# Linear attention and a cosine FFN on one core: keys' maxima subtracted by TensorE in 4 units where it was 7, with a new order table

## The chip, the core and the metric

The kernel runs on one core of a Trainium2 chip. The metric is the device time of one execution in microseconds (us). The kernel before takes 993.45 us, the median of 3 runs (992.97 to 993.52).

## The reference, cut to what matters

```python
def phi(x):                                    # q, k: 8 x 8 x 576 x 64, w_phi: 64 x 128
    proj = einsum('bhsd,df->bhsf', x, w_phi)
    proj = proj - max(abs(proj), axis=-1)      # one maximum for each row of 128 features
    return concatenate([exp(proj), exp(-proj)])
kv  = einsum('bhsf,bhsd->bhfd', phi(k), v);  z = sum(phi(k), axis=2)
out = einsum('bhsf,bhfd->bhsd', phi(q), kv) / (einsum('bhsf,bhf->bhs', phi(q), z) + 1e-6)
x = out, heads side by side                    # 4608 x 512
h = x @ w_in;  g = h * cos(h);  y = g @ w_out  # w_in: 512 x 2048, w_out: 2048 x 512
```

The data are float32. The matmuls of the attention run on float32 as it is (two records of the trace for one matmul); those of the FFN split every operand into a high and a low part and multiply three of the four pairs.

## The kernel before, in words

**Work.** The attention is cut into 32 units (`attention(u)`, L518), each with two heads of one batch. The FFN (`visit`, L795, and `visit_two`, L962) takes 512 rows of x at a time, which four units have to deliver. So nothing of the FFN can start until the first four units are stored and the first weights are converted to their two parts.

**One unit** is a set of steps on the engines:

- PE (TensorE): `q_mm` (L548, two matmuls) and `q_end` (L551) project the queries; `k_mm` (L594, eight matmuls into two banks) and its tail (L619) project the keys; `kv_mm` (L698 and L704) makes kv; two `x_mm` (L733, the second with L739) multiply it by the queries.
- ACT (ScalarE): `q_copy` (L559 twice, L561) empties the query banks; `exp_k` (L649 or L652) and `exp_q` (L658, four instructions) are the exponentials; `kv_out` (L710) copies kv.
- DVE (VectorE): the maxima of the queries (L565 to L574, L583), those of the keys (`k_max`, L632), `k_neg` (L635), and the division and transposition of the result (L745 to L761).
- POOL (GpSimd): the subtraction of the queries' maxima (L579, L587).

**The keys' maxima.** A unit's keys stand in two full banks of 128x512 and a small tail. In a unit of `K_SUMS` (L307) the maximum of the two full banks is subtracted on PE by one more matmul into the bank (`k_sub`, L640, its own shape in the list of shapes), after which one ACT instruction (L649) takes exp of the whole bank, once for +x and once for -x. In all other units there is no `k_sub`: DVE makes the negated maximum (`k_neg`, L635), and ACT subtracts it as a bias. A bias holds for 128 columns alone, so a bank then takes 8 instructions of 128x128 (L652) and not 2 of 128x512. The tail goes by bias in every unit.

```python
597        eqs, eqb = [], []
598        on_pe = (0, 1) if u in K_SUMS else ()
...
640            PE.matmul(out=pv, lhsT=minus, rhs=d["mk", i].unsqueeze(2).broadcast_to([P, n, P]), start=False, stop=True,
641                      skip_group_check=True)
...
647            for s in range(2):
648                if i in on_pe:
649                    ACT.activation(out=e[:, :, s * P:(s + 1) * P], in_=pk, func=AF.Exp, scale=1.0 - 2.0 * s)
650                    continue
651                for g in range(n):
652                    ACT.activation(out=e[:, g, s * P:(s + 1) * P], in_=pk[:, g, :], func=AF.Exp, scale=1.0 - 2.0 * s,
653                                   bias=d["lk" if s == 0 else "mk", i][:, g:g + 1])
...
671            if i in on_pe:
672                kms[i] = Step("PE", 0.86, lambda i=i: k_sub(i), [kms[i]], use=[kb[i], pks[i]], kind="a.k_sub")
673            else:
674                kms[i] = Step("DVE", 0.1, lambda i=i: k_neg(i), [kms[i]], use=[pks[i]], port=True, kind=phase + "k_neg")
```

**Order.** Every piece of work is a `Step`; there are 3839. The table `ORDER` (L89 to L235) lists them by number, and `plan()` (L238) issues them in that order: it alone decides how the steps stand in each engine's queue, and it gives out the eight PSUM banks in turn. Each engine works through its queue in order and waits at an instruction whose inputs or buffers are not free. The costs in the `Step`s do nothing at run time. ACT loads a table whenever it goes from exp to sin or back (ACT_TABLE_LOAD). PE's order mixes four shapes of matmul.

Of the kernel before, what the change touches and what calls it, by code (L numbers as in the profile page):

```python
# [26 lines left out]
def phi_attention_then_cos_ffn(ctx: ExitStack, tc: tile.TileContext, qkT, vS, w_phi, w_in, w_out, out, outT):  # L27
# [42 lines left out]
    class Step:  # L70
        def __init__(self, eng, cost, fn, deps=(), take=(), use=(), lat=None, table=None, port=False, kind="", pipe=0.0):
# [10 lines left out]
            for b in self.take + self.use:  # L82
# [6 lines left out]
    ORDER = [0, 3, 5, 4, 7, 8, 6, 9, 42, 58, 10, 11, 1, 44, 59, 46, 18, 60, 1265, 45, 64, 23, 61, 65, 66, 12, 48, 62, 17, 63, 19, 21, 13, 1266, 47, 24, 20, 68, 22,  # L89
# [148 lines left out]
    def plan():  # L238
# [6 lines left out]

        for x in (steps[i] for i in ORDER):
            for b in x.take:
# [56 lines left out]

    GROUP = 3
    Q_DVE = range(0)
    K_SUMS = range(7)  # L307
    WARM = 7
    WHOLE = 8
    W_POOL = ()  # L310
# [1187 lines left out]
```

## Time and profile before

| | |
|---|---|
| median of 3 runs | 993.45 us (992.97 to 993.52) |
| the profiled execution | 991.67 us, of which the span of its instructions is 989.9 us |
| granted TensorE clock | 1.000 over the span |
| PE busy | 982.2 us, 99% |
| PE weight loads | 796.5 us, 80% |
| DVE busy | 854.8 us, 86% |
| ACT busy | 788.3 us, 80% |
| POOL busy | 203.8 us, 21% |
| DMA | 211.67 MB, 214 GB/s on average |

Read it from the busy shares to the stages: an average of 80% for ACT covers stretches in which it is hardly ever idle and others in which a third of its time is free. The tables by stretch in the section on rows show which. [...]

### The profile page before, as it was taken

The page shows a single profiled execution, that of the slowest core. Times are in us where ns is not written, and L with a number is a line of the kernel's source. Part 1 is how long each engine was busy: PE and PEld are TensorE (multiplying, and loading weights), DVE is VectorE, ACT ScalarE, POOL GpSimd, SP SyncE. Part 2 cuts the span into 40 slices and gives each one's busy share as a digit, 9 for nine tenths or more (in the row PEclk, how much of TensorE's full clock was granted, in tenths as well). Part 3 has the DMA queues.
Part 4 walks back from the last instruction along what each step waited for, and adds up shares of the span by engine and source line. Part 5 has one row for each costly group of instructions (what it writes and reads, how often), then busy time and mean ns, then how long its engine had stood idle before and what let it go on. Part 6 is the DMA issues. An engine that isn't in the chain of part 4 may idle for free.

```text
span 989.9 us, 22350 instructions
## 1 busy us (share of the span) xinstructions
PE 982.2 (99%) x8586; PEld 796.5 (80%) x8586; DVE 854.8 (86%) x1494; ACT 788.3 (80%) x1559; POOL 203.8 (21%) x295
## 2 busy tenths in 40 slices
PE   9999999999999999999999999999999999999998
PEld 6778888888888888887778877788888888888886
DVE  7999999998899987877988679999886899776977
ACT  6899999878678868979998879788867776766663
POOL 4664442323232122201123210222000100000000
PEclk9999999999999999999999999999999999999999
DMA  7766865947587583777665746776566486664665
GB/s 259 211 211 194 264 208 177 339 136 234 191 280 247 181 285 126 237 248 275 214 195 174 227 148 203 231 256 212 179 204 214 151 262 189 242 226 160 181 191 191
DMA packets 118746, 211.67 MB, mean 214 GB/s; under 512 B 18672, under 2 KB 61808, under 8 KB 118640
## 3 DMA queue, kind: packets, MB, share of 16 engines
q1 hardware_dynamic: 118496, 210.18, 65.1%
q8 instruction: 67, 1.10, 0.4%
q14 instruction: 39, 0.32, 0.1%
q10 hardware_dynamic: 144, 0.07, 0.0%
HBM read 149.39 MB, written 60.82 MB: 212 GB/s over the span
## 4 chain that ended last, share of the span: by engine, by line
PE 88%; DVE 6%; ACT 2%; DMA 1%; issue 1%; POOL 1%; SPq 1%; DVEq 0%; ACTq 0%; POOLq 0%
PE bank L1293 22%; PE bank L1090 22%; PE bank L860 12%; PE bank L698 5%; PE bank L733 5%; PE bank L907 4%; PE bank L909 4%; PE bank L908 4%; PE bank L594 3%; PE bank L548 2%; PE bank L704 1%; ACT ek L652 1%; DMA qk<-qkT 1%; PE bank L640 1%; DVE m L565 1%
## 5 line engine op out<-in xcount | busy, mean ns | idle before, releaser
L587 POOL TENSOR_TENSOR pq<-pq,bq 128x288 f32<-128x288 f32 x128 | 122.1, 983 | 111.8 <-DVE bq L583 100.9
L652 ACT ACTIVATE ek<-bank,mk 128x128 f32<-128x128 f32 x464 | 128.1, 406 | 6.7 <-DVE mk L635 5.8
L1293 PE MATMUL bank<-gh,wo_l 128*128 128x512 f32 x336 | 104.8, 393 | 0.2
L1293 PE MATMUL bank<-gh,wo_h 128*128 128x512 f32 x336 | 104.9, 393 | 0.0
L579 POOL COPY m<-m 32x36 f32<-32x36 f32 x96 | 30.1, 314 | 331.7 <-DVE m L574 307.4
L658 ACT ACTIVATE eq<-pq 128x576 f32<-128x576 f32 x128 | 81.1, 711 | 4.4 <-POOL pq L587 3.4
L1202 ACT ACTIVATE g<-g,halfpi 128x512 f32<-128x512 f32 x96 | 67.5, 718 | 18.9 <-DVE g L1199 18.5
L1090 PE MATMUL bank<-xh_t,wi 128*128 128x512 f32 x192 | 75.8, 395 | 0.7 <-ACT bank L1108 0.7
L733 PEld LDWEIGHTS bank<-kv,eq 128*64 128x64 f32 x2048 | 63.8, 138 | 13.1 <-issue 3.9
L1293 PEld LDWEIGHTS bank<-gh,wo_l 128*128 128x128 f32 x336 | 62.3, 188 | 14.5 <-ACT gh L50 1.1
L1293 PEld LDWEIGHTS bank<-gh,wo_h 128*128 128x128 f32 x336 | 62.2, 188 | 13.5 <-issue 0.5
L733 PE MATMUL bank<-kv,eq 128*64 128x65 f32 x2048 | 69.7, 223 | 0.0
L698 PEld LDWEIGHTS bank<-vs,ek 128*64 128x64 f32 x2048 | 62.5, 138 | 8.7 <-issue 2.6
L1199 DVE SCALAR_TENSOR_TENSOR g<-g,hs 128x512 f32<-128x512 int32 x72 | 51.5, 723 | 17.8 <-ACT g L1196 17.3
L1293 PE MATMUL bank<-gl,wo_l 128*128 128x512 f32 x168 | 66.1, 394 | 0.6 <-DVE gl L55 0.6
L698 PE MATMUL bank<-vs,ek 128*64 128x65 f32 x2048 | 66.4, 223 | 0.2 <-DVE g_qk L1209 0.2
L1293 PE MATMUL bank<-gl,wo_h 128*128 128x512 f32 x168 | 65.6, 390 | 0.0
L632 DVE TENSOR_REDUCE mk<-bank 128x4 f32<-128x512 f32 (+1 forms) x96 | 50.6, 542 | 8.3 <-PE bank L594 8.3
L907 PE MATMUL bank<-wo_h,gh 128*128 128x512 f32 x144 | 57.7, 401 | 0.0
L1090 PE MATMUL bank<-xh_b,wi 128*128 128x512 f32 x144 | 57.4, 399 | 0.0
L909 PE MATMUL bank<-wo_h,gl 128*128 128x512 f32 x144 | 56.2, 390 | 0.0
L1090 PE MATMUL bank<-x_raw,wi 128*128 128x512 f32 x144 | 56.1, 390 | 0.0
(189 smaller groups left out, 2663.1 us busy)
## 6 DMA issues: line engine op xcount, KB each, us to landing
wi<-wi_parts SPq DMA_DIRECT2D x18, 1792.0 KB, 7.8
qk<-qkT SPq DMA_DIRECT2D x31, 640.0 KB, 4.7
wo_h<-wo_sums SPq DMA_DIRECT2D x24, 512.0 KB, 3.9
wo_l<-wo_sums SPq DMA_DIRECT2D x24, 512.0 KB, 4.1
x_raw<-xs SPq DMA_DIRECT2D x47, 256.0 KB, 3.8
wi_parts<-wi SPq DMA_DIRECT2D x12, 896.0 KB, 5.9
vs<-vS SPq DMA_DIRECT2D x32, 325.0 KB, 5.3
wo_l<-wo_parts SPq DMA_DIRECT2D x18, 512.0 KB, 5.4
```

What stands on the lines that cost most here:

```text
L587: qeng.tensor_tensor(out=d["pq"][:, c], in0=d["pq"][:, c], in1=d["bq"][:, c], op=ALU.subtract)
L652: ACT.activation(out=e[:, g, s * P:(s + 1) * P], in_=pk[:, g, :], func=AF.Exp, scale=1.0 - 2.0 * s, bias=d["lk" if s == 0 else "mk", i][:, ...
L658: ACT.activation(out=e[:, s, :], in_=d["pq"][:, j * S:(j + 1) * S], func=AF.Exp, scale=1.0 - 2.0 * s)
L698: PE.matmul(out=acc[c:c + 64, n, i, :], lhsT=e[:, s, P * n + c:P * n + c + 64], rhs=vs[b["v"].slot][:, 2 * s + i, :], start=(s == 0 and i ...
L733: PE.matmul(out=ps[64 * h:64 * h + 64, 65 * g:65 * g + 65], lhsT=d["eq", j][:, n, c:c + 64], rhs=d["kv"][:, 2 * n + j, :], start=h not in ...
L860: PE.matmul(out=bank(b), lhsT=w[:, part, 2 * r + kt // 2, kt % 2 * P:(kt % 2 + 1) * P], rhs=d.get(("from", kt), d)[x, kt], start=(k == 0), ...
L907: PE.matmul(out=a, lhsT=gh[:, t], rhs=w[:, 0, r], start=first, stop=False)
L909: PE.matmul(out=a, lhsT=gl[:, t], rhs=w[:, 0, r], start=False, stop=last)
L1090: PE.matmul(out=bank(bank_b), lhsT=w[:, part, block, j * P:(j + 1) * P], rhs=d[x, name, j], start=start and k == 0, stop=k == 5, skip_grou ...
L1199: DVE.scalar_tensor_tensor(out=n["g"], in0=n["g"].bitcast(I32), scalar=-TWO_PI, in1=m[key], op0=ALU.mult, op1=ALU.add)
L1202: ACT.activation(out=n["g"], in_=n["g"], func=AF.Sin, bias=halfpi, scale=1.0)
L1293: PE.matmul(out=bank(out[j]), lhsT=w[:, place, part, j * P:(j + 1) * P], rhs=n[x], start=start and i == mine[0] and q == 0, stop=i == mine ...
```

## The change

`K_SUMS` goes from `range(7)` to `range(4)`. In units 4, 5 and 6 the six `k_sub` matmuls (two records each) go; six `k_neg` come on DVE; and ACT's twelve instructions of 128x512 become 48 of 128x128. All 3839 steps stay, and all of the computation. The table `ORDER` is replaced as a whole, so the order on every engine changes.

```diff
-    ORDER = [0, 3, 5, 4, 7, 8, 6, 9, 42, 58, 10, 11, 1, 44, 59, 46, 18, 60, 1265, 45, 64, 23, 61, 65, 66, 12, 48, 62, 17, 63, 19, 21, 13, 1266, 47, 24, 20, 68, 22,
...
+    ORDER = [0, 3, 5, 4, 7, 8, 6, 9, 10, 11, 42, 59, 43, 64, 58, 60, 65, 68, 1, 12, 44, 46, 62, 17, 45, 21, 61, 47, 18, 48, 19, 63, 16, 22, 1265, 49, 66, 50, 1266,
...
-    K_SUMS = range(7)
+    K_SUMS = range(4)
```

**Place 1: PE, the first key subtractions.** `mk` is the tile of the maxima, `minus` the negated unit matrix, `bank` a PSUM bank with its number. Before, the subtractions of units 0 and 1 stand with a projection of eight matmuls between the first and the second:

```order
L640 MATMUL bank3_72<-mk_148,minus_85 128x512
L594 MATMUL bank1_70<-wphi_79,qk_111 128x128
L594 MATMUL bank5_74<-wphi_79,qk_111 128x128
...
L640 MATMUL bank4_73<-mk_165,minus_85 128x512
L640 MATMUL bank1_70<-mk_176,minus_85 128x512
L640 MATMUL bank5_74<-mk_178,minus_85 128x512
```

In the change:

```order
L551 MATMUL bank1_70<-qk_130,wphi_79 128x128
L640 MATMUL bank4_73<-mk_144,minus_85 128x512
L619 MATMUL bank3_72<-wphi_79,qk_111 128x128
L640 MATMUL bank5_74<-mk_158,minus_85 128x512
L640 MATMUL bank2_71<-mk_169,minus_85 128x512
L640 MATMUL bank0_69<-mk_175,minus_85 128x512
L698 MATMUL bank6_75<-vs0_88,ek_183 64x65 x16
```

The eight matmuls have moved ahead of the first subtraction; between the first and the second only one short tail is left.

**Place 2: PE, from the keys to the first matmul of the FFN.** `xh` and `wi` are operands of the FFN's first matmuls (L860). Before:

```order
L551 MATMUL bank5_74<-qk_998,wphi_79 128x128
...
L698 MATMUL bank1_70<-vs0_88,ek_1193 64x65 x16
L698 MATMUL bank1_70<-vs0_88,ek_1229 64x65 x16
L704 MATMUL bank1_70<-vs0_88,ek_948 64x130 x4
...
L619 MATMUL bank6_75<-wphi_79,qk_1109 128x128
L860 MATMUL bank5_74<-xh_b11_815,wi_314 128x512
```

In the change (the first row is where the count of the prediction begins, the row of L619 with `bank3_72` is where it ends):

```order
L551 MATMUL bank1_70<-qk_342,wphi_79 128x128
...
L551 MATMUL bank7_76<-qk_1063,wphi_79 128x128
L619 MATMUL bank3_72<-wphi_79,qk_1189 128x128
L619 MATMUL bank4_73<-wphi_79,qk_1063 128x128
L698 MATMUL bank6_75<-vs1_89,ek_1244 64x65 x16
L698 MATMUL bank6_75<-vs1_89,ek_1298 64x65 x16
L704 MATMUL bank6_75<-vs1_89,ek_1146 64x130 x4
L860 MATMUL bank7_76<-xh_b11_755,wi_334 128x512
```

The first FFN matmul now stands straight behind a kv product, and a key tail stands ahead of that product, in a bank (`bank3_72`) that ACT's exp must have read before.

**Place 3: ACT, the same stretch in the change.** `pq` is the copy of the query projection, `eq` and `ek` the exponentials, `kv` the copy of kv:

```order
L561 ACTIVATE pq_434<-bank1_70 128x2x64
L559 ACTIVATE pq_434<-bank5_74 128x512
L658 ACTIVATE eq_482<-pq_282 128x576 x2
...
L710 ACTIVATE kv_1229<-bank1_70 128x260
L652 ACTIVATE ek_1244<-bank7_76,mk_1106 128x128 x8
L377 ACTIVATE wi_t0_1257<-wi_raw_979 128x1024
L652 ACTIVATE ek_1298<-bank3_72,mk_1191 128x128 x8
L559 ACTIVATE pq_1322<-bank6_75 128x512
```

Before, the exponentials of the keys of units 4 to 6 are rows of L649, two to a bank; now they are rows of L652, eight to a bank, and the last of them, `ek_1298`, is what frees `bank3_72` for the tail of place 2.

## Rows read from the trace of the kernel before

**Rows 1.** The page: busy time, share of the span and instructions of each engine; then the view of PE's waits over the whole span: who waited for whom, us in total, times, longest.

```profile
PE 982.2 (99%) x8586; PEld 796.5 (80%) x8586; DVE 854.8 (86%) x1494; ACT 788.3 (80%) x1559; POOL 203.8 (21%) x295
...
PE bank L1430 <- DVE warm L292: 1.1, 1, 1.1
PE bank L1090 <- ACT bank L1108: 0.7, 1, 0.7
PE bank L1293 <- DVE gl L55: 0.6, 2, 0.3
```

**Rows 2.** The table by stretch: from and to (us), length, then busy us (and instructions) of PE, PE's weight loads, DVE, ACT and POOL, then granted clock, DMA share and GB/s.

```profile
0.00:50.00 50.00, 48.36 (x774) 35.70 (x776) 42.51 (x83) 37.05 (x74) 26.23 (x46) 1.00 0.71 232
50.00:100.00 50.00, 49.98 (x864) 39.68 (x858) 49.10 (x104) 49.37 (x111) 27.48 (x44) 1.00 0.65 201
100.00:150.00 50.00, 49.82 (x692) 41.03 (x687) 48.01 (x95) 49.83 (x123) 22.57 (x31) 1.00 0.75 234
...
160.00:450.00 290.00, 290.00 (x2348) 238.83 (x2347) 252.43 (x410) 231.93 (x435) 73.47 (x100) 1.00 0.67 223
450.00:990.00 540.00, 534.00 (x3871) 433.66 (x3869) 453.02 (x794) 410.19 (x803) 53.92 (x77) 1.00 0.64 207
```

**Rows 3.** PE in order of time (start, length, line, operation, tiles, count of records; in brackets the idle time ahead and who ended it): places where `k_sub` stands, with the row behind each.

```profile
9.01 1.10 PE L640 MATMUL bank<-mk,minus 128*128 128x512 f32 x2 [0.22 <-DVE mk L632]
10.03 1.16 PE L594 MATMUL bank<-wphi,qk 64*128 64x128 f32 x16
11.23 2.84 PE L640 MATMUL bank<-mk,minus 128*128 128x512 f32 x6
...
35.13 2.74 PE L640 MATMUL bank<-mk,minus 128*128 128x512 f32 x6
37.80 1.13 PE L548 MATMUL bank<-qk,wphi 64*128 64x512 f32 x4
```

**Rows 4.** ACT in order of time, the same columns.

```profile
49.62 0.62 ACT L50 ACTIVATE xh_b<-x_raw 128x512 fp32r<-128x512 f32 x1
50.14 0.27 ACT L561 ACTIVATE pq<-bank 128x128 f32<-128x128 f32 x1
50.29 0.60 ACT L559 ACTIVATE pq<-bank 128x512 f32<-128x512 f32 x1
50.77 2.41 ACT L658 ACTIVATE eq<-pq 128x576 f32<-128x576 f32 x4
53.06 2.06 ACT L649 ACTIVATE ek<-bank 128x512 f32<-128x512 f32 x4
54.97 0.64 ACT L559 ACTIVATE pq<-bank 128x512 f32<-128x512 f32 x1
...
62.81 0.39 ACT L710 ACTIVATE kv<-bank 128x260 f32<-128x260 f32 x1
63.08 0.64 ACT L50 ACTIVATE xh_b<-x_raw 128x512 fp32r<-128x512 f32 x1
...
65.66 1.22 ACT L377 ACTIVATE wi_t<-wi_raw 128x1024 f32<-128x1024 f32 x1
66.71 2.66 ACT L658 ACTIVATE eq<-pq 128x576 f32<-128x576 f32 x4
69.28 2.15 ACT L652 ACTIVATE ek<-bank,mk 128x128 f32<-128x128 f32 x8
71.28 0.43 ACT L710 ACTIVATE kv<-bank 128x260 f32<-128x260 f32 x1
```

**Rows 5.** PE in order of time: one kv product, one set of query and key projections, and both x parts.

```profile
59.67 2.09 PE L698 MATMUL bank<-vs,ek 128*64 128x65 f32 x64
...
62.13 1.13 PE L548 MATMUL bank<-qk,wphi 64*128 64x512 f32 x4
63.19 0.49 PE L551 MATMUL bank<-qk,wphi 128*128 128x128 f32 x2
63.51 1.02 PE L640 MATMUL bank<-mk,minus 128*128 128x512 f32 x2
64.47 1.15 PE L733 MATMUL bank<-kv,eq 128*64 128x65 f32 x32
65.55 1.16 PE L594 MATMUL bank<-wphi,qk 64*128 64x128 f32 x16
66.64 1.15 PE L733 MATMUL bank<-kv,eq 128*64 128x65 f32 x32
...
67.86 2.04 PE L698 MATMUL bank<-vs,ek 128*64 128x65 f32 x64
```

**Rows 6.** DVE in order of time, the first maxima of the keys.

```profile
9.24 1.36 DVE L583 STREAM_TRANSPOSE bq<-m 128x1152 f32<-128x1152 f32 x1
10.54 1.98 DVE L632 TENSOR_REDUCE mk<-bank 128x4 f32<-128x512 f32 x3
```

**Rows 7.** DVE, the view of groups by line and shape: busy us, mean ns of one, idle before.

```profile
L635 DVE TENSOR_SCALAR mk<-mk 128x4 f32<-128x4 f32 x50 | 8.5, 178 | 0.7
```

**Rows 8.** A hand-over from PE to ACT, in order of time: the row of PE that stands behind the last L704, and ACT's row that waited for L704.

```profile
47.90 1.13 PE L548 MATMUL bank<-qk,wphi 64*128 64x512 f32 x4
...
48.08 0.39 ACT L710 ACTIVATE kv<-bank 128x260 f32<-128x260 f32 x1 [0.22 <-PE bank L704]
```

292 rows, old and new, of the table ORDER are left out of this document.

## The prediction

> **What bounds the kernel now.** I read the busy shares first, then PE's waits [rows 1]: PE is busy 99% of the span, and the view finds it idle for others in few places; the three largest groups come to 2.4 us, 1.1 of it at the start. So the kernel lasts as long as PE's work, and PE's work is worth its full time wherever nothing else is late. Next I read the table by stretch [rows 2], which the average of 80% for ACT hides: from 50 to 150 us ACT is busy 99.2 of 100 us (49.37 and 49.83) and DVE 97.1, while PE still hardly waits. Before 50 us ACT is free for 13 us (37.05 busy of 50), and after 160 us it is again free a fifth of the time (231.93 of 290, 410.19 of 540). So there are two bounds: PE over the whole, and ACT in the attention-heavy stretch up to 160 us, where the two run level. The change takes work from PE and puts work on ACT in just that stretch. For a finer measure than busy time I compared each interval between two starts on PE with the usual one between the same two lines. By that count PE loses 13 us in the whole span, 2.8 of them up to 162 us.
>
> **PE's work.** Six `k_sub` go. Three of them in a row take 37.80 - 35.13 = 2.67 us, so 0.89 each with a share of the changes of shape, and 0.86 from one to the next [rows 3]: 6 x 0.86 = 5.2 us. The order has 286 changes between the shapes of matmul where it had 289, of other kinds too; pair by pair, at the intervals that the trace has for each, the whole program of PE is 5.6 us shorter. I take 5.6, and 5.2 as the lower end. If PE never waited, that would be the gain.
>
> **ACT's work.** A bank by `k_sub` takes two instructions, 0.955 us (53.06 to 54.97 for four); a bank by bias takes eight, 2.00 us (69.28 to 71.28) [rows 4]. That is 1.04 us more for each of six banks, 6.3 us, all ahead of 70 us. Six ACT_TABLE_LOADs fewer are left in the new order, but all of them past 160 us, where ACT has time to spare [rows 2]: nothing. Six `k_neg` at 0.18 us [rows 7] are 1.1 us on DVE in its own full stretch, hidden as long as ACT is the later of the two; I take nothing, and 1.1 as the upper bound.
>
> [...]
>
> **Where the order makes them meet.** Take the stretch of the new order from the end of L551 on `bank1_70` to the tail L619 on `bank3_72`, which may not start until `ek_1298` has read that bank (places 2 and 3). ACT has to do, from the copy L561 that waits for the first to the end of `ek_1298`: 5 of L561 at 0.15, 9 of L559 at 0.48, 20 of L658 at 0.573, 74 of L652 at 0.25, 4 of L649 at 0.478, 5 of L710 at 0.27, 2 of L377 and 3 of L50 on tiles of the same size at 1.05, and 3 small ones of L50 at 0.52 [rows 4]. That is 45.1 us, and 44.7 at the usual interval of each kind over the whole trace. PE has in the same stretch 5 kv products at 2.46, 5 L548 at 1.06, 5 L551 at 0.32, 5 key projections at 1.09, 4 tails of the size of L551 at 0.32, 6 first x parts at 1.08, 6 second ones at 1.22 and 2 `k_sub` at 0.96 [rows 5]: 41.7 us. Where rows of one shape follow each other the change of shape of about 0.1 us isn't paid; pair by pair it is 40.2. So PE comes to that tail 44.7 - 41.7 = 3.0 us early, 4.5 by the finer count, and waits. I take 4.5. Before, no such loop has ACT's part longer than PE's.
>
> From there to about 153 us of PE's own work the two stay level: 86.3 us of PE against 86.5 of ACT, so 0.15 us are added and nothing is given back. Only then does ACT get ahead again.
>
> Three things come on top. **At the start** (place 1) the second `k_sub` follows the first after a tail of 0.33 us, but its maximum stands behind the transposition of 1.30 us and takes 0.6 [rows 6]. PE is through with the first `k_sub` and the tail after 0.86 + 0.32 = 1.2 us, the maximum there only some 2.0 us after the first `k_sub` could start, as before from 9.01 to 11.23, where a key projection of 1.2 us filled the time [rows 3]. That is 0.85 of wait, between nothing and 1. **Hand-overs**: from the start of the matmuls behind the last L704 to ACT's start 48.08 - 47.90 = 0.18 us [rows 8], and a little less the other way: 0.3, an estimate. **ACT is slower in company**: in the 100 us from 50 to 150 us its instructions, at the shorter intervals of their kinds (lower quartile), add up to 96.5. Of the 3.5 missing 0.8 is idle [rows 2]; the other 2.7, 2.7%, is instructions that take longer, as L658 with 2.57 for four where it is 2.29 elsewhere [rows 4]. Over 44.7 + 86.5 = 131 us that is 3.5 us. Ends: 0 and 4.6 (all of 3.5 in 100).
>
> **The sum.** PE's lateness at 153 us: 4.5 + 0.15 + 0.85 + 0.3 + 3.5 = 9.3 us. The kernel before has lost 2.8 at the point with as much work left. So 6.5 us of new waits stand against 5.6 us of work taken away: +0.9 us. Past 160 us I take PE's losses as they are; the places where PE's own next work covers a hand-over with less than 1.6 us to spare are 114 before and 119 now, by the order. The profiled execution has 989.9 us of span and 1.8 around it, 991.67, which is 1.8 below the median. The difference is carried to the median: 993.45 + 0.9 = **994.4 us**, no change that can be told, since a measurement of this kernel tells about 0.2% (2 us) from no change.
>
> **Rivals.**
> - *ACT uses its free time, and PE keeps its gain (faster).* For: ACT is free for 13 us before 50 us [rows 2], part of it waiting for PE, and PE now has less there. If ACT runs the stretch at its short intervals (3.5 us less) and the later waits go on as they are: 993.45 - 2.6 = 990.9. With the 3.0 of the coarse count instead of 4.5: 989.4. Against: the 2.7% holds over the whole 100 us. It decides if PE's lateness at 153 us is below 9.3 - 2.9 = 6.4 us.
> - *The later waits shrink (faster).* PE loses about 5 us in single gaps past 160 us, of which the view shows L1090 <- ACT 0.7 and L1293 <- DVE 0.6 [rows 1]. An order with more room there would give most of it back: 994.4 - 4 = 990.4. For: the order is new everywhere. Against: 114 and 119 tight places.
> - *ACT and PE wait for each other in turn (slower).* Between 70 and 150 us of the new order PE has no room towards ACT, and ACT none towards PE: of the first matmuls of the FFN ACT's copy (L867) waits, while the kv products wait for ACT's exp. Then each round trip adds its two hand-overs, 0.3 us, and not one in all. About ten trips (two for each kv product) make 3 us: 997.4; with the 4.6 of ACT's slowness 998.5. It decides once ACT's busy share from 70 to 150 us falls below 97%.
> - *The change does little at all*: a PE that was waiting at the six `k_sub` would lose nothing by keeping them. Against: the view shows one wait of 0.2 us at L640 [rows 3].
>
> **How the numbers follow.** The forecast (992 to 995.4) has 0.42. Slower by over 0.2%, above 995.4: the rival of round trips 0.25, and the forecast's own sum with ACT's slowness at its upper end, 0.08: 0.33. Faster by over 0.2%, below 991.5: 0.13 for the first rival, 0.12 for the second: 0.25. The range reaches from the first rival's far end, 989.4, to 998.8, the third's far end with DVE's 0.3 of the 1.1 us; beyond are about 1 in 10 on either side.
>
> **What would show it.** Right: rows of L640 fall from 28 to 16, those of L652 rise from 464 to 512; PE's busy time falls by about 5 us while new waits PE <- ACT (L652, L559, L710) and PE <- DVE (L755) stand between 45 and 155 us, with some 6 to 7 us of lost time; ACT is busy 97% or more from 45 to 155 us, and less idle before 50 us than 13. Wrong: PE idle less than 3 us up to 155 us (then the loop is looser than counted), ACT with idle time from 70 to 150 us (then it is the round trips), or a changed loss past 160 us.

## The result and the profile after

The change takes 998.59 us (median of 4 runs, 998.32 to 1000.72) against 993.21 us for the kernel before (4 runs, 991.97 to 993.52): slower, ratio 1.0060 with an interval of 1.0048 to 1.0072, or 5.4 us. The time lies inside the range that was given, 989.4 to 998.8, but the forecast was 994.4, no change that can be told.

The page of the change, which answers to the first row of [rows 1], and the view of PE's waits over its whole span (who waited for whom, us in total, times, longest):

```profile
PE 981.8 (99%) x8574; PEld 798.9 (80%) x8574; DVE 859.2 (86%) x1500; ACT 789.1 (79%) x1589; POOL 206.8 (21%) x295
```

```profile
PE bank L619 <- ACT ek L652: 2.4, 1, 2.4
PE bank L551 <- ACT ek L652: 2.0, 3, 1.2
PE bank L1430 <- DVE warm L292: 1.1, 1, 1.1
PE bank L733 <- ACT kv L710: 1.0, 2, 0.9
PE bank L594 <- ACT ek L652: 0.8, 1, 0.8
PE bank L1090 <- ACT bank L1108: 0.8, 1, 0.8
PE bank L733 <- ACT eq L658: 0.7, 2, 0.5
PE bank L640 <- DVE mk L632: 0.6, 1, 0.6
```

PE has twelve records fewer and is busy as long as before (981.8 against 982.2): a matmul at a lower clock counts as busy (2.00 of 2.00 us from 78 to 80 us at a clock of 0.57, below), and so does one whose two records start apart (at 396.51 us the four records of L548 take 1.72 us and not 1.13, the second record starting 0.53 us after the first, where it started 0.01 us after it at 4.42 us in the kernel before). But for those of L1430 and L1090, which stood there before, the waits in the view are new or longer, and nearly all of them name ACT. The largest stands at the tail that the prediction named. The table by stretch, in the columns of [rows 2]:

```profile
0.00:50.00 50.00, 47.47 (x787) 35.51 (x789) 42.05 (x84) 40.55 (x94) 27.87 (x46) 1.00 0.60 199
50.00:100.00 50.00, 45.48 (x804) 37.15 (x802) 47.97 (x105) 47.38 (x125) 23.33 (x39) 0.97 0.69 213
100.00:150.00 50.00, 49.37 (x670) 40.59 (x668) 48.50 (x88) 48.91 (x121) 18.82 (x27) 1.00 0.72 239
...
160.00:450.00 290.00, 287.89 (x2326) 235.67 (x2325) 255.31 (x406) 227.14 (x427) 75.01 (x100) 1.00 0.68 228
```

From 50 to 100 us PE falls from 49.98 to 45.48, the clock to 0.97, and ACT, which should have become the full engine, falls too, from 49.37 to 47.38. Counted as in the prediction (each interval between two starts on PE less the usual one between the same two lines, always by the kernel before), PE's loss grows like this, in us (worked out from the starts of PE's instructions, and printed by no view; how the usual interval is taken moves single figures by up to 1 us ahead of 160 us and 2 us past it, and the differences between the two kernels by 0.6):

| up to | 40 us | 80 us | 160 us | the end | past 160 us |
|---|---|---|---|---|---|
| before | 0.8 | 1.3 | 2.8 | 13.0 | 10.2 |
| the change | 1.8 | 9.5 | 12.7 | 25.3 | 12.6 |
| forecast for the change | | | 9.3 | | as before |

The loss is 12.3 us larger, PE's work 5.6 smaller: 6.7 us, and the spans differ by 996.7 - 989.9 = 6.8. The medians differ by 5.4, since the profiled execution of before is 1.5 below its median and that of the change (998.4) close to its own.

The chain behind the wait of 2.4 us, in order of time with the columns of [rows 3]: PE, then ACT, then DVE.

```profile
74.35 0.40 PE L739 MATMUL bank<-kv,eq 128*64 128x65 f32 x8
74.68 0.49 PE L551 MATMUL bank<-qk,wphi 128*128 128x128 f32 x2
77.58 0.71 PE L619 MATMUL bank<-wphi,qk 128*128 128x128 f32 x4 [2.40 <-ACT ek L652]
78.22 3.66 PE L698 MATMUL bank<-vs,ek 128*64 128x65 f32 x64
```

```profile
72.76 1.53 ACT L377 ACTIVATE wi_t<-wi_raw 128x1024 f32<-128x1024 f32 x1
75.35 2.17 ACT L652 ACTIVATE ek<-bank,mk 128x128 f32<-128x128 f32 x8 [1.06 <-DVE mk L635]
```

```profile
71.38 0.67 DVE L632 TENSOR_REDUCE mk<-bank 128x4 f32<-128x512 f32 x1
71.98 0.80 DVE L755 TENSOR_TENSOR rb<-bank,dn 128x256 f32<-128x256 f32 x2
72.71 1.35 DVE L583 STREAM_TRANSPOSE bq<-m 128x1152 f32<-128x1152 f32 x1
74.00 0.64 DVE L55 TENSOR_TENSOR xl_b<-x_raw,xh_b 128x512 fp32r<-128x512 f32 x1
74.57 0.75 DVE L635 TENSOR_SCALAR mk<-mk 128x4 f32<-128x4 f32 x1
```

PE waits for ACT, ACT has waited 1.06 us for DVE's `k_neg`, and DVE has not been idle at all. (This exponential is that of unit 7, which went by bias before as well; the words on place 3 put it with units 4 to 6.) Behind the wait the kv product takes 3.66 us where it took 2.09 [rows 5]. The table by stretch, its last columns the granted clock, the DMA share and GB/s, shows why:

```profile
76.00:78.00 2.00, 0.42 (x3) 0.42 (x4) 1.97 (x7) 2.00 (x8) 1.55 (x3) 1.00 0.45 89
78.00:80.00 2.00, 2.00 (x37) 1.88 (x37) 1.99 (x8) 2.00 (x7) 0.00 (x0) 0.57 0.75 174
80.00:82.00 2.00, 2.00 (x42) 2.00 (x40) 1.93 (x3) 2.00 (x6) 0.00 (x0) 0.57 0.67 174
82.00:84.00 2.00, 2.00 (x14) 1.50 (x11) 2.00 (x3) 2.00 (x9) 0.00 (x0) 1.00 0.06 8
```

After the idle time the granted clock is 0.57 in each of the two stretches from 78 to 82 us (0.50 from 79 to 81 us), and 1.00 again from 82 us on. At (1 - 0.57) x 4 that is 1.7 us, and by the count of intervals 1.9. All four executions of the change were granted 0.996 to 0.998 over the span, and no recorded one of the kernel before less than 0.999.

### The profile page after: what moved, and what is told of

It reads as the page before. It is cut to its first block, busy times and chain, and to the rows that moved or that the text cites. A ratio compares the mean times of both kernels' runs of the same rounds, so it can differ in the third digit from the quotient of the medians.

```text
span 996.7 us, 22351 instructions
## 1 busy us (share of the span) xinstructions
PE 981.8 (99%) x8574; PEld 798.9 (80%) x8574; DVE 859.2 (86%) x1500; ACT 789.1 (79%) x1589; POOL 206.8 (21%) x295
## 4 chain that ended last, share of the span: by engine, by line
PE 62%; DVE 16%; ACT 14%; DMA 4%; issue 3%; SPq 0%; POOL 0%; DVEq 0%; ACTq 0%; POOLq 0%
PE bank L1090 20%; PE bank L1293 20%; PE bank L860 6%; PE bank L698 3%; ACT ek L652 3%; PE bank L733 3%; DVE gl L55 2%; PE bank L594 2%; PE bank L548 2%; ACT eq L658 2%; ACT g L888 1%; PE bank L907 1%; PE bank L908 1%; PE bank L909 1%; DMA qk<-qkT 1%
## 5 line engine op out<-in xcount | busy, mean ns | idle before, releaser
L652 ACT ACTIVATE ek<-bank,mk 128x128 f32<-128x128 f32 x512 | 143.3, 420 | 6.5 <-DVE mk L635 6.1
L579 POOL COPY m<-m 32x36 f32<-32x36 f32 x96 | 32.5, 338 | 317.0 <-DVE m L574 312.1
L1090 PE MATMUL bank<-xh_t,wi 128*128 128x512 f32 x192 | 75.7, 394 | 1.0 <-ACT bank L1108 0.8
L1199 DVE SCALAR_TENSOR_TENSOR g<-g,hs 128x512 f32<-128x512 int32 x72 | 49.2, 693 | 16.3 <-ACT g L1196 15.6
L1090 PE MATMUL bank<-xh_b,wi 128*128 128x512 f32 x144 | 57.4, 399 | 0.0
L1090 PE MATMUL bank<-x_t,wi 128*128 128x512 f32 x144 | 56.2, 390 | 0.0
L1090 PE MATMUL bank<-x_raw,wi 128*128 128x512 f32 x144 | 56.1, 390 | 0.0
```

The costliest lines, as they stand in the source:

```text
L1090: PE.matmul(out=bank(bank_b), lhsT=w[:, part, block, j * P:(j + 1) * P], rhs=d[x, name, j], start=start and k == 0, stop=k == 5, skip_grou ...
L1199: DVE.scalar_tensor_tensor(out=n["g"], in0=n["g"].bitcast(I32), scalar=-TWO_PI, in1=m[key], op0=ALU.mult, op1=ALU.add)
```

## The experiments

They ask three things: which half of the change costs the time, which engine PE waits for up to 160 us, and what the low clock and the places past 160 us are worth. All ratios are to the kernel before, which ran again beside each of three groups of kernels (medians 993.19, 993.71 and 993.31 us); a difference in us across groups carries that half a us.

### Each half alone

```diff
 (the change)          -    K_SUMS = range(4)     +    K_SUMS = range(7)      new_order_7
 (the kernel before)   -    K_SUMS = range(7)     +    K_SUMS = range(4)      old_order_4
```

> The new order table with the old K_SUMS = range(7): the order without the other half of the change. Theory A (ACT's 6.3 us of added work make PE late; the order itself is as good): PE has 6.2 us more work than in the change, and its waits from 40 to 80 us (6.4 us, with the 1.9 us of the low clock after them) go; so 996 to 997. Theory B (the order costs something whatever K_SUMS is: the late first subtraction, 0.9 us, and the 2.4 us more that PE loses after 160 us): 993.2 + 0.6 + 0.9 + 2.4 = 997, and PE's waits past 160 us stay as they are in the change (L551 <- ACT L652 1.2 us near 405 us). Theory C (the order is good and K_SUMS is all): no slower than before, 993.

Measured: 997.90 us, ratio 1.0051 (1.0039 to 1.0063). PE lost 4.0 us up to 80 us and 6.6 up to 160, but 12.3 past 160 us, as in the change.

> The order table of before with K_SUMS = range(4). PE has 5.0 us less work, ACT 6.3 us more. Theory A (ACT): in the old order ACT's added work stands in the same stretch up to 80 us, PE waits for ACT there by 6 to 9 us: 995 to 998, and no loss added past 160 us. Theory C (the order makes the loss, not K_SUMS): a gain of up to 5 us, 988 to 990.

Measured: 1001.27 us, ratio 1.0080 (1.0063 to 1.0098). PE lost 12.0 us up to 80 us.

So the order costs 4.7 us with the old `K_SUMS`: theory C falls in both kernels, and theory B, though 0.9 short in time, has the place past 160 us. With the new order the six `k_sub` are worth nothing: putting back 6.2 us of PE's work leaves the time where it was (0.7 us less, and the intervals overlap), since waits go with them. With the old order the change of `K_SUMS` costs 8 us. Theory A has the place there, since the waits name ACT (L652), but the time is 3 us past its range. From 20 to 78 us neither DVE nor ACT is full in that kernel (51.27 and 52.51 us busy of 58, PE 50.76), so an order that was not made for its `K_SUMS` makes PE wait without a full engine too. The old pair is the best of the four; the new order is no better with its own `K_SUMS` than with the old one.

### ACT's six microseconds taken away

```diff
-                if i in on_pe:
+                if i in on_pe or i < 2 and u in (4, 5, 6):
                     ACT.activation(out=e[:, :, s * P:(s + 1) * P], in_=pk, func=AF.Exp, scale=1.0 - 2.0 * s)
```

> The change, but in units 4, 5 and 6 the exponential of a full bank of keys is taken of the whole bank (2 instructions of 128x512, as for a bank with k_sub) and without the bias: the subtraction of the maximum is left out there; k_neg and everything else stay. ACT has 6.3 us less to do, PE and DVE the same as in the change. Theory A (ACT is what PE waits for up to 80 us): the 6.4 us of waits between 40 and 80 us shrink to under 1, the clock does not fall after them (1.9 us): 990 to 991. Theory D (DVE is as full as ACT there, 9.9 of 10 us in every slice from 20 to 80 us, and comes next): the waits change their name from ACT to DVE (L755, L635) and stay at 5 us or more: 997 to 999.

Measured: 998.60 us, ratio 1.0054 (1.0041 to 1.0067): nothing gained. The table by stretch from 20 to 78 us, of the kernel before, of the change and of this one, each in a fence (busy us of PE, PE's weight loads, DVE, ACT, POOL):

```profile
20.00:78.00 58.00, 57.77 (x1111) 44.38 (x1110) 56.75 (x119) 52.05 (x118) 36.37 (x54) 1.00 0.73 224
```

```profile
20.00:78.00 58.00, 52.78 (x1090) 42.05 (x1090) 56.80 (x124) 54.38 (x145) 37.11 (x54) 1.00 0.65 204
```

```profile
20.00:78.00 58.00, 52.25 (x1090) 41.56 (x1089) 56.80 (x124) 48.50 (x108) 37.34 (x54) 1.00 0.64 203
```

ACT now idles 9.5 of 58 us and PE still waits for it: PE's loss up to 80 us is 9.4 where it was 9.5. DVE's column is the one that doesn't move: 56.75, 56.80, 56.80. It was as full before the change as after it. What ACT waits for in this kernel, from 20 to 80 us, is first of all DVE (4.8 us in the two largest rows; 2.0 us name PE, 2.3 POOL):

```profile
ACT ek L652 <- DVE mk L635: 2.4, 3, 1.4
ACT wo_h L50 <- DVE wo_t L418: 2.4, 1, 2.4
```

Theory A, the forecast's own, falls. Theory D has the time, and DVE behind ACT, but not the names: from 20 to 80 us PE's waits still name ACT, all but 0.2 us (DVE's L755).

### DVE's work cut, alone and with ACT's

```diff
-            DVE.tensor_reduce(out=m, in_=pv, axis=AX.X, op=ALU.max, apply_absolute_value=True)
+            DVE.tensor_reduce(out=m, in_=pv[:, :, 0:P // 2] if i < 2 and 2 <= u < 10 else pv, axis=AX.X, op=ALU.max, apply_absolute_value=True)
```

The deep cut has this as well, and POOL's subtraction reads the half that is made:

```diff
-            DVE.transpose(out=d["bq"], in_=d["m3"].unsqueeze(2).broadcast_to([P, 4 * NJ, 32]))
+            n = 2 if 2 <= u < 10 else 4; DVE.transpose(out=d["bq"][:, 0:n * HALF], in_=d["m3"][:, 0:n * NJ].unsqueeze(2).broadcast_to([P, n * NJ, 32]))
```

> The change, but in units 2 to 9 the keys' maximum (L632) of a full bank is taken over 64 of the 128 features: half of the input of 16 instructions, which leaves that half out of the maximum. If half the input takes half of the 0.57 us, DVE has 4.5 us less to do between 20 and 110 us; ACT and PE have the same as in the change. Theory D1 (DVE alone is what PE waits for there): 4 us of PE's waits go, the low clock with them: 993 to 994.5. Theory D2 (DVE and ACT are both full, and either alone holds PE back): 997 to 998.6, with the waits on ACT as they are.

Measured: 995.61 us, ratio 1.0019 (1.0011 to 1.0028): 3.0 us less than the change (4.1 by the two ratios), between the two theories.

> The change with both cuts: whole banks without bias on ACT in units 4 to 6 (6.3 us less on ACT) and half the maxima's input on DVE in units 2 to 9 (4.5 us less on DVE). Theory D2 (two full engines, each as late as the other): now PE's waits from 40 to 80 us fall from 6.4 to some 2 us and the clock stays up: 992 to 993.5. Theory E (no engine's total counts, but single hand-overs that the order places too tight, above all the exponential behind L377 in front of the key tail near 77 us): that wait of 2.4 us stays within 0.5 us, and the low clock with it: 996 to 998.

Measured: 995.56 us, ratio 1.0019 (1.0010 to 1.0027): no better than DVE's cut alone, and 2 us short of what theory D2 expected. From 20 to 78 us DVE was busy 56.14 of 58 us in spite of the cut, so this kernel could not tell the theories apart: its DVE was still full. Hence the deeper cuts:

> The change, with the halved maxima of dve_half and with L583 in units 2 to 9 made over half of its columns (the second head is then subtracted the maxima of the first, its own are left out): some 0.65 us less for each of eight units, so DVE has another 5 us less to do up to 110 us. ACT and PE as in the change. Theory D1 (PE is held back by DVE alone): another 2 to 3 us are gained on dve_half, 992.5 to 993.5. Theory D2 (ACT is next, as full as it is): as dve_half, 995 to 996, and ACT busy 9.9 of 10 us and more from 30 to 100 us with DVE below 9.5.

Measured: 995.59 us, ratio 1.0021 (1.0012 to 1.0030).

> The same cuts on DVE as in dve_deep, and ACT's whole banks without bias in units 4 to 6. Theory D2: now neither is full: PE's loss up to 80 us falls from 9.5 (the change) and 5.5 (both_cut) to under 4, and the time to 993 or 994; what stays is the first subtraction (0.8 us), the 12.5 us past 160 us, and the waits between 85 and 125 us, which belong to ACT's part of the FFN. Theory E (single tight places whatever the engines have to do): the waits near 48, 63 and 74 us stay as in both_cut (0.7, 1.0 and 1.9 us), 995 to 996.

Measured: 993.13 us, ratio 0.9999 (0.9990 to 1.0008). From 20 to 78 us, dve_deep and then both_deep:

```profile
20.00:78.00 58.00, 54.76 (x1151) 43.98 (x1146) 52.30 (x130) 56.33 (x152) 36.54 (x54) 1.00 0.68 212
```

```profile
20.00:78.00 58.00, 55.90 (x1171) 45.32 (x1171) 55.15 (x133) 53.00 (x121) 37.10 (x54) 1.00 0.69 216
```

With DVE freed (52.30) ACT is the full one (56.33), and the second cut of DVE brings nothing on top of the first: D2, not D1. With both cut PE goes from 54.76 to 55.90 and the time falls by another 2.5 us, though DVE is still busy 55.15 of 58. PE's loss up to 80 us runs 9.5, 6.0, 4.2 from the change over dve_deep to both_deep (under 4 was expected). So in the new order two engines hold PE back, and each hides the other: ACT's cut is worth nothing while DVE is full and 2.5 us once it is not.

> The kernel before (old order, K_SUMS = range(7)) with the same two cuts on DVE as in dve_deep. A control: PE lost 2.8 us up to 160 us there, so if PE is what bounds it, DVE's 9 us less can give at most some 2 us, and more likely under 1: 992 to 993.5. If DVE holds the kernel before back too, as it does the change: 988 to 990.

Measured: 993.31 us, ratio 1.0000 (0.9991 to 1.0008). The control: the same cuts gain nothing in the kernel before, where PE lost 2.3 us up to 80 us with them. There PE is the bound, and DVE keeps up uncut, at 56.75 us of 58.

### The one place near 77 us

```diff
 ORDER = [
-... 308, 276, 277, 278, 279, 345, 242, 243, 299, 312, 1560, 331, 1302, 309, ... 332, 313, ...
+... 308, 309, 276, 277, 278, 279, 345, 242, 243, 299, 312, 313, 1560, 331, 1302, ... 332, ...
```

> The change with two numbers of the order table moved: unit 7's second k_neg to just behind its maximum on DVE (it runs at 74.57 us in the change, and ACT idles 1.06 us for it), and the exponential that needs it ahead of L377 on ACT (1.05 us). All of the computation stays. Theory E (that one place costs the wait of 2.4 us and the low clock of 1.9 us): the tail waits 0.3 us, 994.5 to 995. Theory D2 (the engines' totals hold PE back): the tail waits for DVE's L755 next, 1 to 1.5 us are gained by PE there and part of them lost again by 100 us: 996.5 to 998.

Measured: 998.23 us, ratio 1.0048 (1.0035 to 1.0062): a little above what D2 expected, and theory E falls. The six executions come in two kinds: three at a granted clock of 1.000 over the span (997.16 to 997.81 us) and three at 0.997 or 0.998 (998.65 to 999.76), so a low clock is worth about 2 us here; at 1.000 the kernel is inside D2's range and still 2 us above theory E's. The first tail no longer waits, but the next tail and a kv product do:

```profile
75.06 0.49 PE L619 MATMUL bank<-wphi,qk 128*128 128x128 f32 x2
76.64 0.49 PE L619 MATMUL bank<-wphi,qk 128*128 128x128 f32 x2 [1.09 <-DVE rb L755]
...
92.66 0.66 PE L704 MATMUL bank<-vs,ek 128*64 128x130 f32 x8 [1.81 <-issue]
```

> Both cuts and the two moved numbers together. Theory D2: like both cuts alone, or 0.5 us better: 991.5 to 993. Theory E: the moved numbers take 3.5 to 4 us off what the two cuts leave: 992 to 994. What PE loses past 160 us (12.6 us in the change) is not touched by any of it, and should stay between 12 and 13.

Measured: 995.89 us, ratio 1.0023 (1.0014 to 1.0032), no better than both_cut and outside what either theory gave. PE lost 5.2 us up to 80 us, but 4 us more between 90 and 100 us, at the same L704 and at a low clock behind it (0.83 from 90 to 100 us). What that L704 waited for, the trace does not name in this kernel; in both_cut and both_deep it names ACT's cosine (L888) for 1.33 and 1.32 us at the same place.

### The low clock

```diff
+        fill_at = steps[385]
         for x in plan():
+            if x is fill_at:
+                for _ in range(10):
+                    PE.matmul(out=banks[7][:, 3 * P:4 * P], lhsT=warm, rhs=warm, start=True, stop=True, skip_group_check=True)
             x.fn()
```

> The change, with ten matmuls of 128x128 on a tile of zeros (0.22 us each, 2.2 us in all, into columns of a bank that nobody reads) on PE in front of the key tail that waits 2.4 us near 77 us. They lie inside that wait, so PE's own work is not later for them. Theory K (the low clock of 78 to 82 us, granted 0.57, follows from the idle time ahead of it): the granted clock stays at 1.00, the kv product behind it takes 2.1 us and not 3.7, and the time falls by 1.9 us to 996.7. Rival (the clock falls for another reason, or the waits before 60 us are enough): same time as the change, 998.6, clock low again.

Measured: 997.21 us, ratio 1.0039 (1.0027 to 1.0051), 1.4 us less than the change; the intervals of the two ratios touch. In the profiled execution:

```profile
54.00:56.00 2.00, 1.17 (x20) 0.90 (x16) 1.90 (x5) 2.00 (x9) 1.79 (x4) 1.00 0.98 343
56.00:58.00 2.00, 2.00 (x17) 1.59 (x16) 1.84 (x8) 2.00 (x7) 2.00 (x4) 0.67 0.86 305
58.00:60.00 2.00, 2.00 (x30) 1.78 (x32) 2.00 (x4) 2.00 (x6) 1.77 (x3) 0.50 0.31 87
78.00:80.00 2.00, 2.00 (x62) 1.88 (x62) 1.83 (x7) 2.00 (x7) 0.00 (x0) 1.00 0.84 186
```

Behind the filled wait the clock stays at 1.00, as expected. But in this execution it falls at 56 us instead, behind waits that stand there in the change too (PE idle for 0.50, 0.24 and 0.83 us between 53 and 56 us). And the execution of late_maximum (below), which is the change unaltered up to 400 us, has the same picture with nothing filled: low from 56 to 60 us, then a wait of 1.54 us at L619 (shorter than the 2.40 of the change) with 1.00 behind it. The wait of 2.03 us at the same tail in new_order_7 is not followed by a low clock either:

```profile
56.00:58.00 2.00, 2.00 (x15) 1.78 (x16) 1.84 (x6) 2.00 (x7) 2.00 (x3) 0.55 0.97 359
78.00:80.00 2.00, 2.00 (x68) 1.91 (x62) 2.00 (x6) 2.00 (x6) 0.00 (x0) 1.00 0.81 222
```

```profile
76.98 0.71 PE L619 MATMUL bank<-wphi,qk 128*128 128x128 f32 x4 [1.54 <-ACT ek L652]
```

```profile
79.12 0.71 PE L619 MATMUL bank<-wphi,qk 128*128 128x128 f32 x4 [2.03 <-ACT ek L652]
79.77 2.09 PE L698 MATMUL bank<-vs,ek 128*64 128x65 f32 x64
```

(The first two fences are late_maximum, the third is new_order_7.) So every low clock seen before 160 us follows waits of PE, at one place or another, but not every such wait brings one, and this run does not show that the filling kept the clock up: theory K is not decided by it. The 1.9 us are the price in the profiled execution of the change, which has one low stretch and 0.998 over the span; the other three were granted 0.996 to 0.998. The low clock is not what makes the new order slow with the old `K_SUMS`: new_order_7 was granted 1.000 in all five executions.

### A place past 160 us

```diff
 ORDER = [
-... 2099, 2100, 2101, 750, 2130, 2084, 776, 777, 782, ...
+... 2099, 776, 777, 2100, 2101, 750, 2130, 2084, 782, ...
```

> The change with two numbers of the order table moved, at 400 us: unit 19's first k_max and k_neg go on DVE ahead of the multiplication L891 that waits 0.79 us for ACT's cosine; in the change they stand behind it, ACT's table load waits 1.08 us for them, and PE's L551 waits 1.34 us at 405.6 us for the bank that the exponential frees. All of the computation stays. Theory L (what PE loses past 160 us comes from such single places of the new order): that wait goes, PE's loss past 160 us falls from 12.6 to 11.3 us and the time by 1.2 us, to 997.4. Rival (the wait moves to the next matmul that needs a bank): no change, 998.6.

Measured: 997.01 us, ratio 1.0037 (1.0023 to 1.0051), 1.6 us less than the change (1.2 expected); the intervals of the two ratios touch, so the place itself has to carry it. PE's loss past 160 us fell from 12.6 to 11.0. ACT in the change, then PE in late_maximum:

```profile
402.06 1.28 ACT L652 ACT_TABLE_LOAD   x1 [1.08 <-DVE mk L635]
```

```profile
403.96 0.49 PE L551 MATMUL bank<-qk,wphi 128*128 128x128 f32 x2
```

In the change L551 stood at 405.58 with 1.18 us of idle time in front of it. Theory L holds for this place, where two numbers of the table take the wait away; that the rest of the loss past 160 us is made of such places was not tried.

## Why the prediction was wrong

**Right.** The counts, in the view of groups by line and shape of the change (busy us, mean ns | idle before, who ended it):

```profile
L640 PE MATMUL bank<-mk,minus 128*128 128x512 f32 x16 | 8.3, 619 | 0.6 <-DVE mk L632 0.6
L652 ACT ACTIVATE ek<-bank,mk 128x128 f32<-128x128 f32 x512 | 143.3, 420 | 6.5 <-DVE mk L635 6.1
```

The second row tells more than its count: of the 6.5 us that ACT idles ahead of L652, 6.1 end with DVE's `k_neg`. PE has 5.6 us less work, and it keeps none of it. The stretch and the place: PE first gets late between 45 and 78 us, and the largest wait is that of L619 on `bank3_72`. The first subtraction: 0.9 us of loss from 10 to 20 us where 0.85 was forecast. And the size up to 160 us: 12.7 us, less 1.9 of low clock and 1.0 of a slow start (below), is 9.8 where 9.3 was forecast.

**The step that failed in its reasoning** is "hidden as long as ACT is the later of the two; I take nothing", and with it the whole view of two bounds. The rows showed a third: DVE busy 49.10 and 48.01 in the two stretches of 50 us [rows 2], which the text read and then dropped. Before the change DVE was full (56.75 of 58) and PE without waits, while ACT had 6 us free (52.05). After it DVE is as full, and its cut alone is worth 3.0 us (dve_half). That the sum came near 9.3 with ACT's figures alone is luck: act_whole takes 5.9 us of ACT's work away and PE's loss up to 80 us stays at 9.4; dve_deep shows that DVE alone was not the cause either. And the forecast put nearly all of its new waits on ACT, but new_order_7, which has none of ACT's added work, is 4.7 us slower than the kernel before. That 5.6 us taken from PE alone would be worth nothing in the old order, where DVE has no time in hand, is an argument; no run took them from PE without giving work to ACT and DVE.

**The step that failed in size** is "6.5 us of new waits": the loss grew by 12.3 (9.9 up to 160 us, 2.4 past it). Four parts make the difference between +0.9 and the 6.8 us of the spans:
- The low clock, 1.9 us: no term of the sum.
- "Past 160 us I take PE's losses as they are": 12.6 us against 10.2, so 2.4. The count of tight places, 114 and 119, gave no reason to expect it. The nine kernels with the new order that leave this part of it unmoved lose 12.1 to 13.2 us there; late_maximum shows one place that is worth 1.6.
- The start, 1.0 us: the first four records of L548 took 2.08 us in the change where they took 1.13. This is chance, not the change: the control old_order_7_deep, with the old order, has 2.08 as well, and both_cut, with the new one, 1.42.
- What is left, about 0.5 us, is inside the loop from 45 to 80 us.

**The rivals.** The first (PE keeps its gain) and the second (later waits shrink) did not happen. The third, the round trips, gave 997.4 and comes nearest in time, and its condition was met, by the table for 70 to 150 us (ACT 77.03 of 80 us, 96.3%, below the 97%):

```profile
70.00:150.00 80.00, 76.71 (x1093) 62.98 (x1091) 77.10 (x150) 77.03 (x190) 29.91 (x48) 0.98 0.74 236
```

But its mechanism is not what happened: from 80 to 150 us PE lost 3.0 us, 0.9 of it at the low clock, and no round trip of 0.3 us was seen ten times; the loss stands ahead of 80 us, in waits of 0.2 to 2.4 us beside a full DVE. The fourth, that the `k_sub` are worth little, came out so in the new order (new_order_7), but not for its reason, waits at L640: these come to 0.6 us. With 0.33 on slower the direction was not left out, only rated too low.

**Open.** How much of the remaining 7.6 us up to 160 us in both_deep is the order and how much the engines was not separated, nor what the L704 near 92 us waits for, nor why some short waits of PE are followed by a low clock and some longer ones are not. Full engines were shown as the cause for the new order with `K_SUMS` of 4 only, by kernels that leave part of the computation out.

## What to carry to other kernels

Before an engine is relieved, ask for every other engine how much idle time it has in that very stretch: work taken from PE can be worth nothing where DVE and ACT arrive with no time in hand. When two engines hold back a third, cutting one of them can show nothing, so cut both before either is ruled out, and look whether the engine that was cut is really idle afterwards. A new wait costs more than its length where the clock falls behind it (in the change 1.9 us on top of a wait of 2.40), and a new order has to be read to its end, past the stretch that it was made for.

## What the runs showed of the hardware

- A wait of PE can be followed by a stretch at a lower granted clock: in the change 2.40 us of wait, then 0.57 over the 4 us from 78 to 82, after which the clock is back at 1.00 while PE works. It need not be: 2.03 us of wait in new_order_7 and 1.81 in exp_early were followed by 1.00.
- The column of the granted clock does not show a slow start: the first L548, at 4.41 us, takes 1.13 us in the kernel before, 1.42 in both_cut and 2.08 in the change and in old_order_7_deep, and the column has 1.00 there in the kernel before, in the change and in old_order_7_deep alike. The traces' own records of the clock tell more: the first one, with a share of 1.00, begins at 4.18 us in the kernel before, ahead of L548, and at 6.62 in the change, behind it; the column has 1.00 ahead of these records too. What the clock was there is not recorded, so the length of the same instruction has to tell. Why it differs, with one program on PE up to there, was not shown. In both_cut:

```profile
4.41 1.42 PE L548 MATMUL bank<-qk,wphi 64*128 64x512 f32 x4
```

- `k_neg`, 0.15 us in the median, took 0.75 us at 74.57 while POOL was at its subtraction, and ended 0.02 us after one of POOL's instructions did. The view of the line in the change (least, median, longest of L635 in ns; first and last start), and POOL in order of time:

```profile
L635 DVE TENSOR_SCALAR mk<-mk x32: 110/154/817, 9.9 to 145.7; 128x4 f32<-128x4 f32 x18, 128x1 f32<-128x1 f32 x14
```

```profile
74.21 3.34 POOL L587 TENSOR_TENSOR pq<-pq,bq 128x288 f32<-128x288 f32 x4 [1.93 <-DVE bq L583]
```

It is not the only one: the kernel before has one such `k_neg` (0.77 us) and the change six (0.62 to 0.82 us), which the forecast's 0.18 us for each left out; every one is of 128x4, and each of the seven ended 0.02 to 0.03 us after the end of a TENSOR_TENSOR of POOL. No run here took POOL away, so the cause is not shown.
